# An output projection over 448 rows instead of 512, with half-row passes of paired token tiles, and the transfers that go with it

## The chip, the cores and the metric

The kernel runs on one NeuronCore of one Trainium2 chip. TensorE (PE) multiplies matrices and writes its results to PSUM, in banks of 128 partitions by 512 floats. ScalarE (ACT), VectorE (DVE) and GpSimd (POOL) do elementwise work, and SyncE (SP) issues almost all DMA transfers. Each engine carries out its own instructions in order, and the engines meet at semaphores. The metric is device time in microseconds (us); lower is better.

## The reference

Two kinds of layers alternate, each applied twice with the same weights, on 2048 tokens of 448 features:

```python
B, S, D, H = 1, 2048, 448, 16          # Dh = D // H = 28
def _A_ref(x, wq, wk, wv, wo):
    q = (x @ wq).reshape(B, S, H, Dh).transpose(0, 2, 1, 3)
    k = x @ wk                          # one key and one value head for all 16
    v = x @ wv
    p = softmax(einsum("bhqd,bkd->bhqk", q, k) * Dh ** -0.5)
    o = einsum("bhqk,bkd->bhqd", p, v)
    return o.transpose(0, 2, 1, 3).reshape(B, S, H * Dh) @ wo
def _B_ref(x, w_gate, w_up, w_down):    # w_gate, w_up: 448 x 1792
    return (silu(x @ w_gate) * (x @ w_up)) @ w_down
x = x + _A_ref(layernorm(x), wq, wk, wv, wo)
x = x + _B_ref(layernorm(x), w_gate, w_up, w_down)
x = x + _A_ref(layernorm(x), wq, wk, wv, wo)
x = x + _B_ref(layernorm(x), w_gate, w_up, w_down)
```

The change concerns the last line of `_A_ref`, the product with `wo`, whose contraction runs over 16 heads of 28 rows, 448 in all.

## The kernel before

**Tiling.** The 2048 tokens are 16 tiles of 128, four of which make a chunk `c` of 512. The 16 heads are four groups `g` of four heads. `xres` holds the residual stream, one 448-wide row per token. Where an operand of a matmul needs float precision it is split into a high and a low half (`split`, L135 and L136: two GpSimd instructions), and a product takes three passes: high by high, high by low, low by high.

**Projection stage** (`Attention.project`, `q`). Per chunk, four products of 11 matmuls give queries, keys and values; 16 such products a layer, numbered by `self.seen` (0 to 15, called the first to the sixteenth below). ScalarE copies each result to a staging tile (L538, L539), SyncE stores it (`qd`, L540; `kt`, L543). `self.plan[n, 0]` and `self.plan[n, 1]` hold steps that are emitted before and after product n, and `self.when[n]` further steps behind it: the loads of keys (`key_load`), the stacking of queries (`stack`, L421) and their halving (`parts`). Before each chunk's first products its normalized input is turned by TensorE (`flip`, L248) and halved. `norm_steps` gives the steps of a normalization: four statistics on VectorE (L217, L218), the reciprocal root on GpSimd (`scale`, L222 and L223), four applications on VectorE (L230). In layer 0 the statistics of chunks 2 and 3 are taken together behind the fifth product (`chunks=2`).

**Attention stage** (`scores`). For each of 16 pairs (chunk, head group), called `i`, there are eight cycles `u`, each of two key tiles. In a cycle TensorE computes the scores of both tiles with four heads side by side in 32-row strips (`tile_scores`, L605): three heads go into a triple of PSUM banks (`threes[0]` for the first tile, `threes[1]` for the second), the fourth into a single bank. ScalarE takes the exponentials out of the triples (L627), VectorE copies the single banks (L626), ScalarE takes the exponentials of these (L628). Then TensorE multiplies the previous cycle's exponentials by the values, four heads in 32-column strips (`pv`, L660), and VectorE adds the result to `accs[i]` (L667 at u = 0, L669 after). A column of ones among the values leaves the softmax sum in row 28 of each head's 32 rows.

**After a group** (`post`). SyncE collects the sums (`rs`, L683). Four cycles later, at u = 3 of the next pair, `rest` takes reciprocals (L691), sends them through DRAM and back to all rows (L693, L694), multiplies on GpSimd (L701), and halves the result into `onh` and `onl`. Here each group has 128 rows, of which 4 x 28 count: the projection contracts 4 x 128 = 512 rows, and `load_wo` places wo in the same layout over zeros.

**Output projection** (`outproj`). For a token tile of 128 there are 4 groups by 3 passes, 12 matmuls of 128 rows by 448 columns (L590). For chunks 0, 1 and 2 this is done between two cycles (`between_cycles`, at u = 6, as soon as the chunk's last group is halved): token tiles 1, 2 and 3 into `threes[0]`, then three additions to `xres` (L594), then tile 0 into a single bank and its addition. For chunk 3 it follows the attention stage, between the first units of the feed-forward: `rest` is called behind `unit(0, 0, 0)`, three groups are projected ahead of the remaining step of the down product, the last group after it.

**Feed-forward** (`FeedForward.unit`). Per chunk and 128 hidden features: two products into two of the banks 0 to 3 (`LOW`), silu on ScalarE (L953), a product on VectorE (L954), halving (L955, L958), and the down product (`down`) in 64-row halves side by side (`side_by_side`, L332).

**Between the layers** (`hand_over`). In the last group of units each chunk is normalized for layer 1, turned on VectorE (L268), sent to DRAM (L274), loaded in the other layout (L882 to L885) into two of the three query stacks `qts`, free at that time, and halved. For chunk 2 the halving stands in `plan[6, 0]` of layer 1.

A variant of `forward` for large scores (`full`) is compiled too and runs only if a check of the sums fails.

Of the kernel before, what the change touches and what calls it, by code (L numbers as in the profile page):

```python
# [55 lines left out]
def forward(  # L56
# [84 lines left out]
    halfn = pers.tile([P, 8], F32, name="halfn")  # L141
# [69 lines left out]
    def norm_steps(c, pool=pers, twice=True, chunks=1):  # L211

        got = {}
        cs = slice(4 * c, 4 * c + 4 * chunks)
# [5 lines left out]
        def scale():  # L220
            rstd = pers.tile([P, 4 * chunks], F32, name=f"rstd{chunks}", bufs=2)
            nc.gpsimd.tensor_scalar(rstd, mv[:, cs, 1], 1.0, EPS, ALU.mult, ALU.add)  # L222
            nc.gpsimd.tensor_tensor(rstd, rstd, halfn[:, 0 : 4 * chunks], ALU.pow)  # L223
            got["r"] = rstd
# [9 lines left out]
        fs = [lambda t=t: stat(t) for t in range(4 * chunks)] + [scale]  # L234
# [108 lines left out]
    class Attention:  # L343
# [222 lines left out]
        def scores(self, ff, xb):  # L566
            next(switch)
            inner = ExitStack()
            with tc.tile_pool(name=f"ow{self.layer}", bufs=1, side="right", reuse_waits="tile") as ow:
# [4 lines left out]
                on, accs, pts = {}, {}, {}  # L574
                todo, due, late = [], {}, []

                def load_wo(z):
                    r = wpool.tile([P, 4, 2, P], F32, name="wr").rearrange("p (z k) b n -> p z (k b n)", z=2)
                    nc.gpsimd.memset(r, 0.0)
                    for j in range(4):  # L580
                        nc.sync.dma_start(r[32 * j : 32 * j + DH, :, 0:D], wos[j][:, 2 * z : 2 * z + 2, :])
                    zs = slice(2 * z, 2 * z + 2)
                    split(woh[:, zs, :], wol[:, zs, :], r[:, :, 0:D])

                def outproj(c, t, po, gs=range(NG)):
                    oh, ol = on[c]
                    ts_ = slice(P * t, P * t + P)
                    for g in gs:
                        for z, (a, b) in enumerate(((oh, woh), (oh, wol), (ol, woh))):
                            nc.tensor.matmul(  # L590
                                po[:, 0:D], a[:, g, ts_], b[:, g, :], start=(g + z == 0), stop=(g == NG - 1 and z == 2)
                            )
                    if gs[-1] == NG - 1:
                        return lambda: nc.vector.tensor_tensor(  # L594
                            xres[:, 4 * c + t, :], po[:, 0:D], xres[:, 4 * c + t, :], ALU.add
                        )
# [38 lines left out]
                def between_cycles(m):  # L635
# [7 lines left out]
                    if not todo or u != 6:  # L643
                        return
                    c = todo.pop()
                    one = singles(m)[1]
                    adds = []
                    for t in (1, 2, 3):
                        adds.append(outproj(c, t, threes[0][:, t - 1, :]))
                    for f in adds:  # L650
                        f()
                    outproj(c, 0, one)()

                def pv(m, to):
# [18 lines left out]
                    if u == NT // 2 - 1:  # L673
                        due[m + 4] = post(i)

                def post(i):
# [5 lines left out]
                    for j in range(4):  # L682
                        nc.sync.dma_start(rs[32 * j : 32 * j + 32, :], oraw[32 * j + DH : 32 * j + DH + 1, :])  # L683

                    def rest():
# [9 lines left out]
                        if g == 0:  # L695
# [3 lines left out]
                            )  # L699
                        oh, ol = on[c]  # L700
                        nc.gpsimd.tensor_tensor(rb, oraw, rb, ALU.mult)  # L701
# [4 lines left out]
                    return rest  # L706
# [72 lines left out]
                for gs in (range(NG - 1), range(NG - 1, NG)):  # L779
                    for t in range(4):  # L780
                        add = outproj(NC - 1, t, pos[t], gs)
                        if add:
                            add()
                    while ff.left:
# [324 lines left out]
```

## Time and profile before

| what | value |
|---|---|
| median of 3 runs | 1973.64 us (1972.16 to 1973.9) |
| the profiled execution | 1973.03 us, of which the span from first to last instruction is 1971.3 us |
| granted TensorE clock, mean | 0.996 of full speed |
| TensorE busy | 1943.9 us (99%) |
| ScalarE busy | 1260.6 us (64%) |
| VectorE busy | 967.6 us (49%) |
| GpSimd busy | 554.1 us (28%) |
| DMA | 80.50 MB in 99875 packets |
| projection matmuls (L590) | 216 into triples, 168 into single banks |

A timeline row has the start in us from the span's start, the duration in us, the engine, the line of the kernel, the operation, the tile written and the tiles read, and the count; in brackets the engine's idle time before it and what ended that idle time. SPq rows are transfers as SyncE issues them. Rows of the chain of waits have start, duration, and engine or transfer. A row of windows has the stretch, its length, each engine's busy time and count (PE, PEld, DVE, ACT, POOL), the granted clock, the DMA share and GB/s. A matmul's duration is its passage through a pipeline; the distance between the starts of two matmuls is what one costs.

### The profile page before, as it was taken

The numbers are of one execution on the slowest core, as the hardware profiler recorded it, in microseconds if no ns is written. First come the engines' busy times: TensorE is split into PE (matmuls) and PEld (weight loads), VectorE is DVE, ScalarE is ACT, GpSimd is POOL, SyncE is SP. The second block draws the span as 40 slices with busy tenths as digits, with TensorE's granted clock in tenths as the row PEclk, the third lists the DMA queues.
The fourth block names the chain that finished last, engine by engine and source line by source line (L and its number), as shares of the span: only waits on it lengthen the run. The fifth ranks groups of instructions, "written<-read, shape, count | busy, mean of one in ns | idle before, by whom it ended". The sixth has DMA issues, their size and how long they took to land.

```text
span 1971.3 us, 43781 instructions
## 1 busy us (share of the span) xinstructions
PE 1943.9 (99%) x18469; PEld 1340.4 (68%) x18469; DVE 967.6 (49%) x1638; ACT 1260.6 (64%) x1888; POOL 554.1 (28%) x595
## 2 busy tenths in 40 slices
PE   8999999999999999999989999999999999999998
PEld 6644545445458999999965445454454689988886
DVE  6565575665744232322655565656657432222223
ACT  3799798997963333333348997979979433333332
POOL 4313123122214233333332221122221243233320
PEclk9999999999999999999999999999999999999999
DMA  4201002021130111100251010200211300011102
GB/s 152 68 23 33 18 23 52 17 52 32 28 74 22 32 32 32 32 21 23 70 149 40 26 31 12 61 14 23 51 49 26 75 17 27 21 32 32 32 1 77
DMA packets 99875, 80.50 MB, mean 41 GB/s; under 512 B 25848, under 2 KB 82296, under 8 KB 99672
## 3 DMA queue, kind: packets, MB, share of 16 engines
q1 hardware_dynamic: 98120, 76.44, 14.2%
q8 instruction: 146, 2.39, 0.5%
q10 hardware_dynamic: 1552, 1.20, 0.2%
q14 instruction: 57, 0.47, 0.1%
HBM read 56.24 MB, written 20.58 MB: 39 GB/s over the span
## 4 chain that ended last, share of the span: by engine, by line
PE 95%; DVE 1%; DMA 1%; POOL 1%; ACT 1%; issue 1%; SPq 0%; ACTq 0%; POOLq 0%; DVEq 0%
PE bank L332 40%; PE bank L660 24%; PE bank L605 17%; PE three L605 5%; PE bank L312 3%; PE three L590 2%; PE bank L590 2%; PE bank L248 1%; DMA kt<-stage 0%; PE bank L438 0%; DVE stats L217 0%; DMA xd<-xh 0%; POOL vsb L549 0%; DMA xres<-in_A_x_dram 0%; DVE pair L626 0%
## 5 line engine op out<-in xcount | busy, mean ns | idle before, releaser
L627 ACT ACTIVATE pt<-three 128x1536 f32<-128x1536 f32 x512 | 727.2, 1500 | 63.5 <-PE three L605 42.3
L660 PE MATMUL bank<-pt,vsb 128*32 128x512 f32 x3072 | 490.8, 598 | 0.4
L660 PE MATMUL bank<-pair,vsb 128*32 128x512 f32 x1024 | 487.4, 598 | 0.6 <-ACT pair L628 0.6
L605 PE MATMUL bank<-qstack,keys 32*128 32x512 f32 x1536 | 473.1, 424 | 4.3 <-DVE xres L594 4.3
L605 PE MATMUL three<-qstack,keys 32*128 32x512 f32 x4608 | 428.3, 408 | 0.5 <-ACT stage L539 0.3
L605 PEld LDWEIGHTS bank<-qstack,keys 32*128 32x128 f32 x1536 | 243.8, 183 | 255.9 <-issue 123.9
L332 PE MATMUL bank<-xh,wgh 64*128 64x512 f32 x1728 | 405.5, 387 | 0.0
L626 DVE COPY pair<-bank 128x512 f32<-128x512 f32 x512 | 354.3, 692 | 99.3 <-PE bank L605 62.4
L332 PE MATMUL bank<-xh,wgl 64*128 64x512 f32 x1404 | 340.8, 386 | 0.0
L332 PE MATMUL bank<-wdh,h 64*128 64x448 f32 x1792 | 322.4, 362 | 1.4 <-ACT h L955 0.8
L954 DVE TENSOR_TENSOR sg<-bank,sg 128x512 f32<-128x512 f32 x112 | 77.5, 692 | 493.6 <-ACT sg L953 489.4
L332 PE MATMUL bank<-xl,wgh 64*128 64x512 f32 x1296 | 303.3, 386 | 0.0
L628 ACT ACTIVATE pair<-pair 128x1024 f32<-128x1024 f32 x256 | 285.5, 1115 | 0.0
L605 PEld LDWEIGHTS three<-qstack,keys 32*128 32x128 f32 x4608 | 261.2, 183 | 12.7 <-ACT stage L539 0.7
L660 PEld LDWEIGHTS bank<-pt,vsb 128*32 128x32 f32 x3072 | 101.7, 109 | 246.7 <-issue 153.2
L837 POOL TENSOR_TENSOR xres<-stage,xres 128x448 f32<-128x448 f32 x108 | 126.1, 1186 | 495.9 <-ACT stage L836 495.7
L669 DVE TENSOR_TENSOR o<-bank,o 128x512 f32<-128x512 f32 x224 | 155.0, 692 | 204.2 <-PE bank L660 204.2
L339 ACT COPY seen<-bank 128x1 f32<-128x1 f32 x664 | 78.7, 164 | 251.8 <-PE bank L332 250.4
L332 PEld LDWEIGHTS bank<-xh,wgh 64*128 64x128 f32 x1728 | 225.7, 184 | 13.7 <-issue 1.3
L332 PEld LDWEIGHTS bank<-wdh,h 64*128 64x128 f32 x1792 | 217.7, 183 | 13.0 <-issue 2.0
L953 ACT ACTIVATE sg<-bank 128x512 f32<-128x512 f32 x112 | 67.1, 599 | 213.2 <-PE bank L332 210.5
L332 PE MATMUL bank<-wdl,h 64*128 64x448 f32 x896 | 199.1, 364 | 0.0
(134 smaller groups left out, 2193.7 us busy)
## 6 DMA issues: line engine op xcount, KB each, us to landing
o<-rd SPq DMA_DIRECT2D x32, 256.0 KB
qraw<-qd SPq DMA_DIRECT2D x128, 56.0 KB
qd<-stage SPq DMA_DIRECT2D x28, 224.0 KB
wdr<-in_B_w_down_dram SPq DMA_DIRECT2D x28, 224.0 KB
xt<-tb SPq DMA_DIRECT2D x24, 224.0 KB
wr<-in_B_w_gate_dram SPq DMA_DIRECT2D x28, 192.0 KB
wr<-in_B_w_up_dram SPq DMA_DIRECT2D x28, 192.0 KB
xn<-xt SPq DMA_DIRECT2D x6, 768.0 KB
```

The source lines that it names most:

```text
L332: nc.tensor.matmul(po, a, b, start=start, stop=stop, skip_group_check=True)
L339: nc.scalar.copy(seen[:, i : i + 1], po[:, 0:1])
L590: nc.tensor.matmul(po[:, 0:D], a[:, g, ts_], b[:, g, :], start=(g + z == 0), stop=(g == NG - 1 and z == 2))
L605: nc.tensor.matmul(three[:, j, :] if j < 3 else one, k[js, kp, ks], q[js, part, :], start=(z == 0), stop=(z == 2), tile_position=(32 * j, 0),)
L626: copies.append(nc.vector.tensor_copy(pt1, one))
L627: es.append(nc.scalar.activation(pt, threes[y], AF.Exp, scale=SCALE))
L628: es.append(nc.scalar.activation(pair, pair, AF.Exp, scale=SCALE))
L660: nc.tensor.matmul(to[32 * j : 32 * j + 32, :], vsb[:, n % NT, :], pts[n][j], start=(y == 0), stop=(y == 1), skip_group_check=True,)
L669: f = nc.vector.tensor_tensor(accs[i][:, 0, :], to, accs[i][:, 0, :], ALU.add)
L837: nc.gpsimd.tensor_tensor(r, s, r, ALU.add)
L953: nc.scalar.activation(in_order(sg, sq), natural(pg[0], sq), AF.Silu)
L954: nc.vector.tensor_tensor(in_order(sg, sq), natural(pg[1], sq), in_order(sg, sq), ALU.mult)
```

## The change

- **Layout.** Group 0 keeps 64 rows: two of its heads with eight rows in their gaps. The other 56 - 8 = 48 rows of its other two heads go into the gaps (4 of every 32 rows) of groups 1, 2 and 3, which are then full. A copy of group 0's 64 rows stands in partitions 64 to 127. `load_wo` places wo accordingly, row by row range, with 8 transfers per group and without the zero fill.
- **Passes.** `half_rows` takes group 0 for two token tiles at once, one on partitions 0 to 63 and one on 64 to 127, into two banks; `full_rows` takes groups 1 to 3 for one token tile. In `between_cycles` (now at u = 7) the four tiles stand in both triples, two each; the halves of all four come first, then the full rows in an order that alternates between the triples, each tile's addition behind its last matmul.
- **Spreading.** `post` returns three steps instead of one: `rest` (u = 3) up to the multiplication, `spread` (u = 4), which moves the rows by transfers (for group 0 to a DRAM tile `moved` and from there into its own gaps, then the copy of the 64 rows; for the other groups four transfers out of `moved`), and `parts` (u = 6), which halves. At the end of attention `rest` comes ahead of `unit(0, 0, 0)`, `spread` and `parts` behind it. The sums are collected by one transfer instead of four.
- **Layer 0's normalization** is per chunk throughout; chunk 3's statistics come behind product 8.
- **Layer 1's projection.** The turned chunks are loaded into `qts[1]` and `qts[2]` instead of `qts[0]` and `qts[1]`; chunk 2's load moves behind product 4 and its halving from ahead of product 6 to ahead of product 7.

```diff
...
-    def norm_steps(c, pool=pers, twice=True, chunks=1):
+    def norm_steps(c, pool=pers, twice=True):
...
                 def load_wo(z):
-                    r = wpool.tile([P, 4, 2, P], F32, name="wr").rearrange("p (z k) b n -> p z (k b n)", z=2)
-                    nc.gpsimd.memset(r, 0.0)
-                    for j in range(4):
-                        nc.sync.dma_start(r[32 * j : 32 * j + DH, :, 0:D], wos[j][:, 2 * z : 2 * z + 2, :])
+                    r = wpool.tile([P, 4, 2, P], F32, name="wr").rearrange("p (z k) b n -> p z (k b n)", z=2)[:, :, 0:D]
+                    for g in (2 * z, 2 * z + 1):
+                        s_ = r[:, g % 2, :]
...
+                        own = wo[4 * DH * g : 4 * DH * g + 4 * DH, :]
+                        n0 = 2 * DH + 16 * g - 16
+                        for q in range(4):
+                            nc.sync.dma_start(s_[32 * q : 32 * q + DH, :], own[DH * q : DH * q + DH, :])
+                            nc.sync.dma_start(s_[DH + q :: 32, :], wo[n0 + 4 * q : n0 + 4 * q + 4, :])
...
+                def full_rows(c, t, po, gs):
+
                     for g in gs:
-                        for z, (a, b) in enumerate(((oh, woh), (oh, wol), (ol, woh))):
+                        for z, (a, b) in enumerate(passes(c)):
                             nc.tensor.matmul(
-                                po[:, 0:D], a[:, g, ts_], b[:, g, :], start=(g + z == 0), stop=(g == NG - 1 and z == 2)
+                                po[:, 0:D], a[:, g, P * t : P * t + P], b[:, g, :],
+                                start=False, stop=(g == NG - 1 and z == 2), skip_group_check=True,
                             )
...
+                def half_rows(c, ts, pos):
+
+                    for z, (a, b) in enumerate(passes(c)):
+                        for t, po, rs in zip(ts, pos, (slice(0, 64), slice(64, 128))):
+                            nc.tensor.matmul(
+                                po[:, 0:D], a[rs, 0, P * t : P * t + P], b[rs, 0, :],
+                                start=(z == 0), stop=False, skip_group_check=True,
+                            )
...
-                    if not todo or u != 6:
+                    if not todo or u != 7:
                         return
                     c = todo.pop()
-                    one = singles(m)[1]
-                    adds = []
-                    for t in (1, 2, 3):
-                        adds.append(outproj(c, t, threes[0][:, t - 1, :]))
-                    for f in adds:
-                        f()
-                    outproj(c, 0, one)()
+                    order = (1, 2, 3, 0)
+                    pos = [threes[n // 2][:, n % 2, :] for n in range(4)]
+                    for n in (0, 2):
+                        half_rows(c, order[n : n + 2], pos[n : n + 2])
+                    for n in (0, 2, 1, 3):
+                        full_rows(c, order[n], pos[n], range(1, NG))
+                        add_to(c, order[n], pos[n])()
...
-                        due[m + 4] = post(i)
+                        rest, spread, parts = post(i)
+                        due[m + 4], due[m + 5], due[m + 7] = rest, spread, parts
...
-                    for j in range(4):
-                        nc.sync.dma_start(rs[32 * j : 32 * j + 32, :], oraw[32 * j + DH : 32 * j + DH + 1, :])
+                    nc.sync.dma_start(rs, oraw[DH::32, :].rearrange("j (p n) -> j p n", n=16))
...
+                    def spread():
+                        if g == 0:
+                            moved[c] = dram.tile([2 * DH, 512], F32, name=f"moved{self.layer}_{c}")
+                            for q in (0, 1):
+                                nc.sync.dma_start(moved[c][DH * q : DH * q + DH, :], rb[64 + 32 * q : 64 + 32 * q + DH, :])
+                            for q in (0, 1):
+                                n0 = 2 * DH - 8 + 4 * q
+                                nc.sync.dma_start(rb[32 * q + DH : 32 * q + 32, :], moved[c][n0 : n0 + 4, :])
+                            nc.sync.dma_start(rb[64:128, :], rb[0:64, :])
+                            return
+                        n0 = 16 * g - 16
+                        for q in range(4):
+                            nc.sync.dma_start(rb[DH + q :: 32, :], moved[c][n0 + 4 * q : n0 + 4 * q + 4, :])
...
                 ff.begin(xb)
+                due.pop(min(due))()
                 ff.unit(0, 0, 0)
-                due.popitem()[1]()
+                due.pop(min(due))()
                 ff.fetch(2)
+                due.pop(min(due))()
                 ff.unit(0, 0, 1)
-                pos = [bank(LOW)[1] for _ in range(4)]
...
+                c, pos = NC - 1, [bank(LOW)[1] for _ in range(4)]
+                for two in (slice(0, 2), slice(2, 4)):
+                    half_rows(c, range(4)[two], pos[two])
+                for t in range(4):
+                    full_rows(c, t, pos[t], range(1, NG - 1))
+                while ff.left:
+                    ff.left.pop(0)()
+                for t in range(4):
+                    full_rows(c, t, pos[t], range(NG - 1, NG))
+                    add_to(c, t, pos[t])()
...
             if c == 2:
-                a.plan[6, 0] = [parts]
+                a.plan[4, 1] = [load]
+                a.plan[7, 0] = [parts]
                 return
...
-        if c == 2:
-            two = got
-            at.plan[n, 1] = fs[:9]
-        elif c == 1:
-            at.plan[n, 1] = fs[:5]
-        else:
-            at.plan[n, 1] = [lambda got=got: got.__setitem__("r", two["r"][:, 4:8])]
-        at.plan[n + 1, 1] = fs[-4:] + [lambda c=c, got=got: at.norms.__setitem__(c, got)]
+        at.plan[n, 1] = fs[:5]
+        at.plan[n + 1, 1] = fs[5:] + [lambda c=c, got=got: at.norms.__setitem__(c, got)]
```

More of the change, by code (lines that the diff above doesn't have):

```diff
@@ L220, in scale @@
         def scale():
-            rstd = pers.tile([P, 4 * chunks], F32, name=f"rstd{chunks}", bufs=2)
+            rstd = pers.tile([P, 4], F32, name="rstd", bufs=2)
             nc.gpsimd.tensor_scalar(rstd, mv[:, cs, 1], 1.0, EPS, ALU.mult, ALU.add)
-            nc.gpsimd.tensor_tensor(rstd, rstd, halfn[:, 0 : 4 * chunks], ALU.pow)
+            nc.gpsimd.tensor_tensor(rstd, rstd, halfn, ALU.pow)
             got["r"] = rstd
@@ L232, in apply @@
                 nc.gpsimd.tensor_copy(got["x"][:, t, D:512], o[:, 384:D])
-        fs = [lambda t=t: stat(t) for t in range(4 * chunks)] + [scale]
+        fs = [lambda t=t: stat(t) for t in range(4)] + [scale]
         return fs + [lambda t=t: apply(t) for t in range(4)], got
```

50 lines of the change are left out of this document (27 added, 23 removed).

## The prediction

> **What bounds the kernel now.** I read the list of engines first, then the chain that ended last.
>
> ```profile
> PE 1943.9 (99%) x18469; PEld 1340.4 (68%) x18469; DVE 967.6 (49%) x1638; ACT 1260.6 (64%) x1888; POOL 554.1 (28%) x595
> PE 95%; DVE 1%; DMA 1%; POOL 1%; ACT 1%; issue 1%; SPq 0%; ACTq 0%; POOLq 0%; DVEq 0%
> ```
>
> TensorE is the path: 95% of the chain. A change gains by taking slots from TensorE or by closing one of its few holes. So I looked up every place that the diff touches in the timeline and read it there. All durations are from the profiled execution, which took 1973.03 us, 0.6 below the median of 1973.64.
>
> **Part 1: the six projections inside attention.** This is TensorE at the second of them, from its first matmul to the scores behind it.
>
> ```profile
> 337.57 0.47 PE L590 MATMUL three<-woh,onh 128*128 128x448 f32 x1
> 337.88 0.36 PE L590 MATMUL three<-wol,onh 128*128 128x448 f32 x1
> ...
> 347.19 0.37 PE L590 MATMUL bank<-woh,onl 128*128 128x448 f32 x1
> 347.60 0.62 DVE L594 TENSOR_TENSOR xres<-bank,xres 128x448 f32<-128x448 f32 x1 [0.67 <-PE bank L590]
> 348.28 0.49 PE L605 MATMUL bank<-qstack,keys 32*128 32x512 f32 x1 [0.72 <-DVE xres L594]
> ...
> 349.33 2.79 ACT L627 ACTIVATE pt<-three 128x1536 f32<-128x1536 f32 x2 [10.61 <-PE bank L605]
> ```
>
> Starts count here, not durations, because matmuls overlap. 48 matmuls: 0.31 to the second start, 46 steps of (347.19 - 337.88) / 46 = 0.2024, and 1.09 to the scores, 0.72 of it a wait for the last addition. Together 10.71 us. ScalarE stands idle for 10.61 of them, so a shorter projection is a shorter span: ScalarE gives nothing back.
>
> The change runs 64 rows instead of 128 for a quarter of the contraction, two token tiles side by side: 48 slots become 36 full and 6 paired. No row shows a paired slot in this place; the feed-forward's down product has the same shape, and behind it stands a switch from 64 to 128 rows.
>
> ```profile
> 978.08 0.41 PE L332 MATMUL bank<-wdl,h 64*128 64x448 f32 x2
> 978.28 0.41 PE L332 MATMUL bank<-wdh,h 64*128 64x448 f32 x2
> 978.62 0.50 PE L312 MATMUL bank<-xh,wh 128*128 128x512 f32 x1
> 978.96 0.40 PE L312 MATMUL bank<-xl,wh 128*128 128x512 f32 x1
> ```
>
> A pair takes 0.20. The switch takes 0.34 for 0.20, and then 0.34 for the 0.23 of a matmul of 512 columns (10.02 us for 44, quoted in part 4): 0.25 extra, once per projection. The wait of 0.72 goes: the next scores write a triple whose last addition began nine full slots earlier, and a bank that the projection no longer uses. Late next is the other triple: its last addition ends 0.41 + 0.62 = 1.03 after the last matmul's start, and the second tile's scores come about 0.37 + 0.8 = 1.17 after it. That hides it by 0.14; uncovered it costs a few tenths. New length: 0.31 + 40 x 0.2024 + 0.37 + 0.25 = 9.03. Gain 1.68, times six: **10.1 us**. Bounds: 2.8 if pairs take two slots each (6 x 6 x 0.20 back), 11.6 if the switch is free.
>
> **Part 2: the transfers in front of it.** Rows of a group are now spread by SyncE between the product with the reciprocals and the halving, and the projection comes one cycle later.
>
> ```profile
> 199.60 0.49 PE L605 MATMUL bank<-qstack,keys 32*128 32x512 f32 x1
> 205.98 1.28 POOL L701 TENSOR_TENSOR o<-o 128x512 f32<-128x512 f32 x1 [7.83 <-DMA o<-rd]
> 206.87 0.49 PE L605 MATMUL bank<-qstack,keys 32*128 32x512 f32 x1
> 207.35 0.62 POOL L135 TENSOR_SCALAR onh<-o 128x512 fp32r<-128x512 f32 x1
> 208.06 1.29 POOL L136 TENSOR_TENSOR onl<-o,onh 128x512 fp32r<-128x512 f32 x1
> 989.09 2.99 DMA kt<-stage
> 1026.84 5.43 DMA kt<-stage
> 593.02 2.31 DMA xd<-xh
> ```
>
> 199.60 is the start of cycle u = 4 and 206.87 that of u = 6, so a cycle is 3.63. The product ends at 207.3. Four small transfers, 0.5 each to issue and 2.3 to land (the nearest row, xd), end at 211.6; the halving, 1.9, at 213.5. The projection now starts at 214.1, needing the last group 2.7 later. Hidden, with 3 to spare. Behind the waiting SyncE stand the next group's transfers and, in two groups, a load of the normalized input; behind the waiting GpSimd, the next query halves, five cycles away. In the first group of a chunk three transfers follow each other: 207.3 + 5 x 0.5 + 3 x 2.3 + 1.9 = 218.6. Its buffer is needed again at about 221.5, when VectorE copies the next but one group's first sum. Hidden, with 2.9 to spare. Loading wo takes 64 transfers instead of 16 and no memset; nothing waits. This part: **0**.
>
> The Trainium skill, "DMA: Bandwidth & Descriptors", section "Anatomy of one DMA", puts about 2.0 us of fixed cost on each transfer, whatever its size (measured there on the software path). It speaks against splitting as the change does; by it the three take 6 us, still hidden, while the rows above go from 2.3 to 5.4.
>
> **Part 3: the projection of the last chunk, once per layer.** Six slots less are 1.21. But the first halves come at once.
>
> ```profile
> 580.84 0.47 PE L590 MATMUL bank<-woh,onh 128*128 128x448 f32 x1
> 581.76 0.69 DVE L954 TENSOR_TENSOR sg<-bank,sg 128x512 f32<-128x512 f32 x1 [4.15 <-ACT sg L953]
> 589.74 0.47 PE L590 MATMUL bank<-woh,onh 128*128 128x448 f32 x1
> ```
>
> The second pair of tiles writes the banks of the unit just computed, which VectorE frees at 582.45; the pair is due at about 581.4. So 1.1 of 1.21 is a new wait. The reciprocals are now issued ahead of the first unit, which pays for the spread: product at about 582, last group ready at about 589, needed at about 589.6 (589.74, less 1.21, plus 1.1). I take **0.2 us** for both layers; bounds -3 (the chain 1.5 late each time) and 2.4.
>
> **Part 4: the first projection stage.** Normalization of chunks 2 and 3 is no longer joined. That looks like tidying; the trace says otherwise.
>
> ```profile
> 29.01 0.62 DVE L217 BATCH_NORM_STATS2 stats<-xres 128x6 f32<-128x448 f32 x1
> 34.77 0.18 DVE L218 BATCH_NORM_AGGREGATE mv<-stats 128x2 f32<-128x6 f32 x1
> 35.40 1.64 POOL L223 TENSOR_TENSOR rstd<-rstd,halfn 128x8 f32<-128x8 f32 x1
> 37.08 1.78 DVE L230 TENSOR_SCALAR xn<-xres,mv,rstd 128x448 f32<-128x448 f32 x4 [2.13 <-POOL rstd L223]
> 37.65 4.30 PE L248 MATMUL bank<-ident,xn 128*128 128x128 f32 x16 [2.52 <-DVE xn L230]
> 37.60:42.00 4.40, 4.36 (x17) 3.63 (x18) 4.18 (x9) 1.78 (x4) 1.43 (x4) 0.50 0.01 2
> 41.95 10.96 PE bank L312 x44
> 52.91 0.94 PE bank L438 x4
> 53.84 1.75 PE bank L248 x16
> 55.59 10.02 PE bank L312 x44
> ```
>
> Eight tiles of statistics run from 29.01 to 34.95, GpSimd's power follows, and the flips of chunk 2 wait 2.52 for the input that VectorE then normalizes. Meanwhile the granted clock falls to 0.50 (third figure from the end of the window's row): the flips take 4.30 where the next chunk's take 1.75, and 44 matmuls 10.96 instead of 10.02. With four tiles the input is normalized from 37.08 - 2.97 - 0.62 (a smaller power) = 33.5 on, done by 35.3. The wait goes but for 0.3, and with it the slow clock, 2.55 in the flips and 0.94 behind them. What is late next is chunk 3: its four statistics, 3.0, now come after the ninth product. The flips of chunk 3 would be due at about 35.1 + 1.75 + 10.0 + 0.9 = 47.8. On VectorE the statistics stand behind chunk 2's splits and a transpose and end at about 44.7; GpSimd has a key halving ahead of the power, which ends at about 46.6; four normalizations end at 48.4. About 0.4 is lost. Gain 2.2 + 2.55 + 0.94 - 0.4 = **5.3 us**; bounds 2 (the wait less the loss) and 6.
>
> **Part 5: the second projection stage.** The largest hole that I found:
>
> ```profile
> 997.13 0.59 ACT L539 COPY stage<-bank 128x512 f32<-128x512 f32 x1
> 1006.19 0.38 SPq L882 DMA_DIRECT2D qstack<-xt  x1
> 1008.29 1.05 SPq L540 DMA_DIRECT2D qd<-stage  x2
> 1012.38 0.59 ACT L539 COPY stage<-bank 128x512 f32<-128x512 f32 x1 [5.07 <-DMA qd<-stage]
> 1015.45 0.69 DVE L302 TENSOR_TENSOR xh<-qstack,xh 64x512 fp32r<-64x512 f32 x1
> 1017.03 0.76 PE L312 MATMUL bank<-xh,wh 128*128 128x512 f32 x1 [5.75 <-DVE sg L440]
> 1021.03 0.39 PE L312 MATMUL bank<-xh,wh 128*128 128x512 f32 x1
> ```
>
> SyncE waits at chunk 2's load (L882) until the sent chunk has landed, with the fourth product's store, ready at 997.7, behind it until 1008.29. ScalarE therefore gets its staging buffer only at 1012.38, chunk 2's halves are done at 1016.1, and the ninth product, 11 matmuls, runs from 1017.03 to 1021.03, 4.0 instead of 11 x 0.228 = 2.5, since the clock had dropped again. Moved behind the fifth product, the load lets that store out at about 1003 but itself goes out at about 1007.8 instead of 1006.2. It lands near 1012 (2.3 behind the last issue at 1009.8); ScalarE's sixth and seventh copies no longer wait for the late store; VectorE has by then done the maxima that now stand ahead of the halves, and ends at about 1015.5. The products can start on the first rows from 1012.5, so the ninth ends at 1016.1 at full clock, about 1017 if it drops again. I take 1017: **4.0 us**. Bounds: 0 (the later load eats it) and 6.
>
> The Trainium skill, "TensorE: Matmul & The Clock Gate", Part 1, halves the clock only after an idle window of about 3.4 us. By it this shorter hole would not slow the clock and 0.9 more is gained; but the waits of part 4, 2.52 us, were enough for 0.50.
>
> **Sum.** 10.1 + 0 + 0.2 + 5.3 + 4.0 = 19.6, and 1973.03 - 19.6 = 1953.4 in a profiled execution; the median stood 0.6 above that of before, and I give **1953.5**.
>
> **Rivals.**
> - *The spread is late (slower).* One place: the first group of a chunk, eight times. Three transfers in a row have 221.5 - 207.3 - 2.5 - 1.9 = 9.8 us, 3.3 each. Below that nothing; at the 5.43 of the slow store quoted, 6.5 late, with VectorE held in its copy and TensorE's next product behind it: 8 x 6.5 - 20 = 32 slower, 2005. For it: the store at 2.99 is near the limit. Against: loads and copies in this trace land at 2.3 to 2.7. 8%.
> - *The halves do not run side by side:* 8 x 6 x 0.20 = 9.7 back, 1963. Against: the pairs at 978.08. 6%.
> - *The second stage gains nothing:* the load is the late one, 1957.5. 13%.
> - *The chain of part 3 is late:* 3 us, 1956.5. 7%.
> - *More is gained,* clock up throughout and free switches: 1948.5 to 1950. 6%.
>
> **How the numbers follow.** The forecast, with 1950 to 1956 as its own range, has 60%. All rivals but the first end faster: 0.90, since 0.02 goes to a spread so little late that the gain is just eaten, within 0.2% (about what a measurement of this kernel can tell from no change); 0.08 slower. The range reaches to the serial halves above, 1964, and below to all upper bounds at once, 1973 - (11.6 + 2.4 + 6 + 6) = 1947.
>
> **What would show it.** Right: 42 steps of 0.20 and no wait for an addition at the scores; flips of chunk 2 near 35 at clock 1.00; the ninth product of layer 1 ending four earlier relative to its stage. Wrong: VectorE's first copy of a sum waiting for GpSimd; TensorE waiting in the projection for GpSimd's halves; SyncE's late stores now elsewhere in the second stage, with a new hole at a later product.

## The result, and the profile after

The change took the kernel from 1973.64 us to 1962.54 us (medians of six runs each, 1972.08 to 1974.0 and 1961.99 to 1963.64). The ratio is 0.9945, with a 95% interval of 0.9934 to 0.9955. The gain is 11.1 us, where 20.1 had been forecast. The profiled execution after took 1962.25 us with a span of 1960.4. This is its list of engines, and the first line of the chain that ended last:

```profile
PE 1943.3 (99%) x18469; PEld 1325.5 (68%) x18469; DVE 968.3 (49%) x1638; ACT 1264.1 (64%) x1888; POOL 553.6 (28%) x593
PE 87%; ACT 9%; DMA 1%; DVE 1%; issue 1%; POOL 0%; SPq 0%; ACTq 0%; POOLq 0%; DVEq 0%
```

TensorE is still the path. But its busy time has hardly fallen (1943.9 to 1943.3), although each layer's projections have lost slots. Something else on TensorE got longer. A table of leads shows where: for one place in the program after the other, its time from the start of the span in both traces, and how far the changed kernel is ahead.

| place | before | after | lead |
|---|---|---|---|
| first scores, layer 0 | 69.00 | 63.71 | 5.3 |
| first silu of the feed-forward, layer 0 | 572.06 | 561.13 | 10.9 |
| its third silu (last chunk's projection done) | 599.43 | 588.62 | 10.8 |
| its last silu but one | 977.50 | 970.78 | **6.7** |
| first scores, layer 1 | 1042.73 | 1032.85 | 9.9 |
| first silu of the feed-forward, layer 1 | 1545.80 | 1530.39 | 15.4 |
| its third silu | 1573.15 | 1557.89 | 15.3 |
| its last silu | 1958.89 | 1947.76 | **11.1** |
| end of the span | 1971.31 | 1960.42 | 10.9 |

Every stage that the diff touches gains about what was forecast. Both feed-forwards, in which the diff has not changed a line, lose 4.1 us each. The loss is spread evenly. Here are two silus of the feed-forward's units, 29 units apart, in the timeline of ScalarE; first the kernel before:

```profile
761.10 0.60 ACT L953 ACTIVATE sg<-bank 128x512 f32<-128x512 f32 x1 [1.93 <-PE bank L332]
...
970.28 0.60 ACT L953 ACTIVATE sg<-bank 128x512 f32<-128x512 f32 x1 [1.98 <-PE bank L332]
```

and after:

```profile
759.27 0.60 ACT L1006 ACTIVATE sg<-bank 128x512 f32<-128x512 f32 x1 [2.15 <-PE bank L332]
...
970.78 0.60 ACT L1006 ACTIVATE sg<-bank 128x512 f32<-128x512 f32 x1 [1.96 <-PE bank L332]
```

(970.28 - 761.10) / 29 = 7.213 us a unit before, (970.78 - 759.27) / 29 = 7.293 after. Layer 1 has the same two lengths. Some 105 units at 0.08 us are 8.4 us, nearly all of the 9.0 us by which the gain fell short.

Next, the rows of after that answer those shown of before. The second projection inside attention:

```profile
333.97 0.47 PE L621 MATMUL three<-woh,onh 64*128 64x448 f32 x2
334.28 0.36 PE L621 MATMUL three<-wol,onh 64*128 64x448 f32 x2
...
342.60 0.37 PE L612 MATMUL three<-woh,onl 128*128 128x448 f32 x1
342.89 0.50 PE L633 MATMUL bank<-qstack,keys 32*128 32x512 f32 x1
...
343.00 0.62 DVE L604 TENSOR_TENSOR xres<-three,xres 128x448 f32<-128x448 f32 x1 [1.20 <-PE three L612]
343.95 2.79 ACT L655 ACTIVATE pt<-three 128x1536 f32<-128x1536 f32 x2 [8.82 <-PE three L633]
```

From the first pair (x2: both halves in one row) to the scores it is 342.89 - 333.97 = 8.92 instead of 10.71. The scores wait for nothing: the last addition (343.00) runs beside them. ScalarE is idle for 8.82 instead of 10.61.

The first projection stage: VectorE's normalization of chunk 3 and TensorE's flips of chunks 2 and 3, then the granted clock under the flips of chunk 2 (1.00, third figure from the end):

```profile
34.83 2.08 PE L248 MATMUL bank<-ident,xn 128*128 128x128 f32 x16
...
46.37 1.78 DVE L230 TENSOR_SCALAR xn<-xres,mv,rstd 128x448 f32<-128x448 f32 x4 [1.57 <-POOL rstd L223]
47.70 2.15 PE L248 MATMUL bank<-ident,xn 128*128 128x128 f32 x16
```

```profile
34.80:37.00 2.20, 2.20 (x19) 1.94 (x18) 2.06 (x5) 2.20 (x5) 0.71 (x3) 1.00 0.50 158
```

The flips of chunk 2 start 2.8 us earlier, at full clock, and take 2.08 instead of 4.30. Those of chunk 3 take 2.15 instead of 1.75, because the four normalizations end only at 46.37 + 1.78 = 48.15.

The second projection stage, around its ninth product:

```profile
1001.10 0.39 SPq L934 DMA_DIRECT2D qstack<-xt  x1
...
1005.43 1.88 ACT L292 CAST xh<-qstack 128x512 fp32r<-128x512 f32 x3 [2.27 <-DMA qstack<-xt]
1006.10 0.50 PE L312 MATMUL bank<-xh,wh 128*128 128x512 f32 x1 [1.72 <-ACT xh L292]
...
1010.59 0.61 PE L312 MATMUL bank<-xh,wh 128*128 128x512 f32 x1
1011.02 0.42 PE L312 MATMUL bank<-xl,wh 128*128 128x512 f32 x1
...
1024.18 0.50 PE L312 MATMUL bank<-xh,wh 128*128 128x512 f32 x1 [0.47 <-DVE vt L546]
```

TensorE's wait is 1.72 us (5.75 before). The load is now what it waits for. Behind this short wait the matmuls still go at a distance of 0.43 instead of 0.23 until 1011.02 in this execution. The last row is a wait that the kernel before did not have: at the fourteenth product TensorE waits 0.47 us for VectorE's copy of the values (`vt`).

### The profile page after: what moved, and what is told of

Same layout as the page of the kernel before. It is cut to its first block, busy times and chain, and to the rows that moved or that the text cites. A ratio compares the mean times of both kernels' runs of the same rounds, so it can differ in the third digit from the quotient of the medians.

```text
span 1960.4 us, 44004 instructions
## 1 busy us (share of the span) xinstructions
PE 1943.3 (99%) x18469; PEld 1325.5 (68%) x18469; DVE 968.3 (49%) x1638; ACT 1264.1 (64%) x1888; POOL 553.6 (28%) x593
## 4 chain that ended last, share of the span: by engine, by line
PE 87%; ACT 9%; DMA 1%; DVE 1%; issue 1%; POOL 0%; SPq 0%; ACTq 0%; POOLq 0%; DVEq 0%
PE bank L332 40%; PE bank L688 20%; PE bank L633 14%; ACT pt L655 6%; PE three L633 5%; PE bank L312 4%; ACT pair L656 2%; PE three L612 2%; PE bank L612 1%; PE three L621 0%; PE bank L438 0%; DMA kt<-stage 0%; DMA xd<-xh 0%; DMA wr<-in_A_wq_dram 0%; DVE vt L546 0%
## 5 line engine op out<-in xcount | busy, mean ns | idle before, releaser
L332 PE MATMUL bank<-xh,wgh 64*128 64x512 f32 x1728 | 450.7, 389 | 0.0
L332 PE MATMUL bank<-xh,wgl 64*128 64x512 f32 x1404 | 371.7, 391 | 0.0
L332 PE MATMUL bank<-xl,wgh 64*128 64x512 f32 x1296 | 338.1, 390 | 0.0
L332 PE MATMUL bank<-wdh,h 64*128 64x448 f32 x1792 | 334.3, 364 | 1.1 <-ACT h L1008 0.8
L656 ACT ACTIVATE pair<-pair 128x1024 f32<-128x1024 f32 x256 | 281.5, 1100 | 0.0
L332 PEld LDWEIGHTS bank<-xh,wgh 64*128 64x128 f32 x1728 | 266.3, 185 | 16.7 <-issue 1.3
L332 PEld LDWEIGHTS bank<-wdh,h 64*128 64x128 f32 x1792 | 247.5, 184 | 14.8 <-issue 2.0
L332 PEld LDWEIGHTS bank<-xh,wgl 64*128 64x128 f32 x1404 | 219.2, 184 | 13.8
L332 PE MATMUL bank<-wdl,h 64*128 64x448 f32 x896 | 222.2, 367 | 0.0
```

What stands on the lines that cost most here:

```text
L332: nc.tensor.matmul(po, a, b, start=start, stop=stop, skip_group_check=True)
L656: es.append(nc.scalar.activation(pair, pair, AF.Exp, scale=SCALE))
```

## The experiments

**First theory, and its fall.** In the middle of the feed-forward the upper 64 rows run 0.12 us behind the lower ones before the change (starts at 728.21 and 728.33) and 0.20 after (718.65 and 718.85; both streams go through `side_by_side`). I supposed at first that the streams now enter the feed-forward out of step and that this costs 0.08 us a unit. The traces contradict it without a run. In layer 1 the streams fall into step; here is the last pair of a unit before the change and one after it, lower half (xh) and upper half (xd):

```profile
1832.34 0.39 PE L332 MATMUL bank<-xh,wgl 64*128 64x512 f32 x1
1832.34 0.39 PE L332 MATMUL bank<-xd,wgl 64*128 64x512 f32 x1
```

```profile
1863.56 0.39 PE L332 MATMUL bank<-xh,wgl 64*128 64x512 f32 x1
1863.56 0.39 PE L332 MATMUL bank<-xd,wgl 64*128 64x512 f32 x1
```

Both halves start together in both kernels, and the unit there is still 7.21 before (silus at 1829.05 and 1836.26) and 7.29 after (1860.24 and 1867.53). So the distance of the streams doesn't set the length.

**Second theory: placement.** In the feed-forward the instructions, their order and their PSUM banks are the same in both programs. What differs is where the operands lie in SBUF. The joint normalization had a wide tile, `rstd2` (two buffers of 32 bytes a partition); with it gone, everything allocated behind it (silu buffer, feed-forward weights, inputs) lies 64 bytes lower, while the split silu products `h2`, allocated ahead of it, stay. (No trace shows addresses. The 64 bytes follow from the order and the sizes of the allocations; for the second run below they hold only if every tile takes a multiple of 32 bytes.) The theory: this shift makes the unit longer. The rival: something in the way the feed-forward is entered, or the added transfers.

*Putting 64 bytes back, in the changed kernel:*

```diff
             rstd = pers.tile([P, 4], F32, name="rstd", bufs=2)
+            if c == 2:
+                pers.tile([P, 16], F32, name="room")
```

> The changed kernel with 64 bytes a partition of unused SBUF put back where the removed wide normalization tile lay, so that weights, inputs and silu products of the feed-forward lie at the addresses that they had before the change; its instructions stay those of the changed kernel. Placement theory: the feed-forward's unit of work goes back from 7.293 us (changed kernel) to 7.213 us (before) in both layers, and with some 107 units at 0.08 us the time falls by 8.5 us to about 1954. Rival (the unit is longer because of how the two row halves of TensorE enter the feed-forward, or because of the additional transfers, or by where the instructions lie): the unit stays at 7.293 us and the time at 1962.5 within 1 us.

Measured: 1953.85 us (ratio to the kernel before 0.9901, interval 0.9885 to 0.9918).

```profile
757.97 0.60 ACT L1008 ACTIVATE sg<-bank 128x512 f32<-128x512 f32 x1 [2.06 <-PE bank L334]
...
967.16 0.60 ACT L1008 ACTIVATE sg<-bank 128x512 f32<-128x512 f32 x1 [1.93 <-PE bank L334]
```

209.19 / 29 = 7.213. An unused tile, to which no instruction refers, gives 8.7 us.

*Taking 64 bytes away, in the kernel before:*

```diff
-            rstd = pers.tile([P, 4 * chunks], F32, name=f"rstd{chunks}", bufs=2)
+            rstd = pers.tile([P, 8], F32, name="rstd", bufs=2)[:, 0 : 4 * chunks]
```

> The kernel before the change, whose two normalization tiles take one name and together 64 bytes a partition less, so that the feed-forward's tiles lie where the changed kernel has them; nothing else differs. Placement theory: the unit of the feed-forward becomes 7.293 us and the time rises by 8.5 us to about 1982. Rival (entry of the row halves, transfers, instructions): unit 7.213 us, time 1973.6 within 1 us.

Measured: 1981.77 us (1.0044, interval 1.0027 to 1.0061).

```profile
761.65 0.60 ACT L953 ACTIVATE sg<-bank 128x512 f32<-128x512 f32 x1 [1.96 <-PE bank L332]
...
973.15 0.60 ACT L953 ACTIVATE sg<-bank 128x512 f32<-128x512 f32 x1 [2.14 <-PE bank L332]
```

211.50 / 29 = 7.293. The two runs together show the cause: the shift, put back in the one kernel and made in the other, moves the unit between the two lengths, and the times follow. The traces agree slot by slot too: averaged over 19 units, the 33 distances between pairs are the same within 0.001 us in the kernel before and in the changed one with 64 bytes, and again in the changed one and in the kernel before with 64 bytes less; between these two groups some differ by 0.009.

*Other amounts of room* (`[P, 8]` and `[P, 32]` in the first diff):

> The changed kernel with 32 bytes of unused SBUF at that place. Placement theory: another unit length may come out here, since every operand changes its place modulo 64 bytes; if the length follows the place modulo 64 alone, this differs from both lengths seen, and room for 64 bytes would equal none. Rival (not placement): 7.293 us and 1962.5.

> The changed kernel with 128 bytes of unused SBUF at that place. Placement theory with a period of 128 bytes: unit 7.293 us, as without room. Placement theory with a longer period or with the distance to the tiles that do not move (the split silu products): 7.213 us or a third length. Rival (not placement): 7.293 us and 1962.5, told from the first by the run with 64 bytes.

Measured once each: 1964.95 us with 32 bytes, 1952.91 with 128. First 32 bytes, then 128 (the rows are of the later run with the same kernel, 28 units apart):

```profile
760.13 0.60 ACT L1008 ACTIVATE sg<-bank 128x512 f32<-128x512 f32 x1 [2.15 <-PE bank L334]
...
972.41 0.60 ACT L1008 ACTIVATE sg<-bank 128x512 f32<-128x512 f32 x1 [1.97 <-PE bank L334]
```

```profile
757.77 0.60 ACT L1008 ACTIVATE sg<-bank 128x512 f32<-128x512 f32 x1 [2.00 <-PE bank L334]
...
959.37 0.60 ACT L1008 ACTIVATE sg<-bank 128x512 f32<-128x512 f32 x1 [2.00 <-PE bank L334]
```

212.28 / 29 = 7.320 and 201.60 / 28 = 7.200. No period of 64 or 128 bytes: 0 and 128 give different lengths.

*Which distances count.* 64 bytes between the weights and the inputs, and 64 bytes ahead of `h2`, so that everything moves together:

```diff
     xpool = ctx.enter_context(tc.tile_pool(name="xpool", bufs=1))
+    xpool.tile([P, 16], F32, name="room")
```

> The changed kernel with the 64 bytes of unused SBUF put behind the feed-forward's weights and ahead of its inputs: inputs (xh, xl, xd) lie as before the change, weights and silu products as in the changed kernel. If the place of the inputs alone sets the slots, the unit is 7.213 us and the time 1953.9; if the place of the weights alone, 7.293 us and 1962.5; if what counts is the place of one against the other, a third length, such as the 7.32 or 7.20 us that 32 and 128 bytes gave.

```diff
     seen = pers.tile([P, 4], F32, name="seen")
+    pers.tile([P, 16], F32, name="room")
```

> The changed kernel with the 64 bytes put ahead of the split silu products (h2) too, so that everything the feed-forward's multiplications read moves together. If the place in the partition itself counts, it comes out as with room behind h2: 7.213 us and 1953.9. If the distance from the silu products to weights and inputs counts, nothing has changed: 7.293 us and 1962.5.

Measured once each: 1964.18 and 1961.52 us.

```profile
762.65 0.60 ACT L1007 ACTIVATE sg<-bank 128x512 f32<-128x512 f32 x1 [2.13 <-PE bank L333]
...
973.96 0.60 ACT L1007 ACTIVATE sg<-bank 128x512 f32<-128x512 f32 x1 [1.97 <-PE bank L333]
```

```profile
759.15 0.60 ACT L1007 ACTIVATE sg<-bank 128x512 f32<-128x512 f32 x1 [2.14 <-PE bank L332]
...
970.65 0.60 ACT L1007 ACTIVATE sg<-bank 128x512 f32<-128x512 f32 x1 [1.96 <-PE bank L332]
```

Inputs alone: 211.31 / 29 = 7.287, a length of its own (its time is also longer because in that execution TensorE waited 2.92 us at its first product, and the first scores came at 67.29). All together: 211.50 / 29 = 7.293, as without room. So the place itself doesn't count, at least not for 64 bytes: what counts is how far apart the operands lie. Moving the inputs alone gave neither of the two lengths, so more than one distance counts; which ones these runs don't separate.

Where inside a unit is it? TensorE's pairs of one half unit, changed kernel first, then with 64 bytes:

```profile
694.48 0.58 PE L332 MATMUL bank<-xh,wgh 64*128 64x512 f32 x2
...
695.87 0.57 PE L332 MATMUL bank<-xh,wgh 64*128 64x512 f32 x2
...
696.77 0.40 PE L332 MATMUL bank<-xh,wgl 64*128 64x512 f32 x1
```

```profile
693.95 0.52 PE L334 MATMUL bank<-xh,wgh 64*128 64x512 f32 x2
...
695.31 0.52 PE L334 MATMUL bank<-xh,wgh 64*128 64x512 f32 x2
...
696.22 0.39 PE L334 MATMUL bank<-xh,wgl 64*128 64x512 f32 x1
```

The first six slots take 1.39 us against 1.36, the next four 0.90 against 0.91. So most of the excess sits behind the switch from the down product (which reads `h2`) to gate and up, and dies out: two such places make 0.06 of the unit's 0.08 (0.028 each in the average over 19 units), and nearly all of the rest is the slot ahead of each down product (0.237 against 0.228). By what rule a distance lengthens a slot remains open; moving the weights alone wasn't tried.

**The terms of the prediction, one at a time.** All but one of these stand on the changed kernel with 64 bytes of room (1953.85), so that the feed-forward doesn't mix in.

*Halves not side by side:*

```diff
-                        for t, po, rs in zip(ts, pos, (slice(0, 64), slice(64, 128))):
+                        for t, po, rs in zip(ts, pos, (slice(0, 64), slice(0, 64))):
```

> The changed kernel with 64 bytes of room, and both halves of a pair multiplied in the lower 64 rows (the same data lies in both), so that they follow each other instead of lying side by side. By the prediction's reason (42 slots of 0.20 us instead of 48, because six pairs lie side by side) each of the eight output projections gets six slots longer: 8 x 6 x 0.20 = 9.6 us, about 1963.5. Rival (halves were never side by side, the gain came from the alternation of the banks alone): no change, 1953.9.

Measured: 1962.05 us, 8.2 more.

```profile
209.31 0.56 PE L623 MATMUL three<-wol,onh 64*128 64x448 f32 x2
209.72 0.56 PE L623 MATMUL three<-woh,onl 64*128 64x448 f32 x2
```

A pair now takes 0.41 (209.72 - 209.31), and 0.20 side by side (334.28 against 334.48 in the changed kernel). Each attention stage is 3.8 us longer, 1.28 a projection, and each last chunk's projection only 0.4: TensorE waits there for a bank anyway (0.27 and 0.26 with the halves side by side, 0.18 without). The rival falls.

*Full rows triple by triple:*

```diff
-                    for n in (0, 2, 1, 3):
+                    for n in (0, 1, 2, 3):
```

> The changed kernel with 64 bytes of room, and the full rows of the four token tiles taken triple by triple (first both of the one, then both of the other) instead of alternately. If multiplications into one bank of a triple wait until VectorE has added the other bank of it, each of the six projections in attention waits twice for an addition of 0.62 us and its release: 6 x 2 x 0.7 = 8.4 us, about 1962. If waits are kept bank by bank, the additions lie beside the multiplications either way: 1953.9.

Measured: 1966.24 us, 12.4 more, all of it in attention (6.2 and 6.5 us). The longest line in TensorE's list of waits (us in total, times, longest), and one of the waits:

```profile
PE three L614 <- DVE xres L606: 9.4, 12, 0.8
```

```profile
340.04 0.62 DVE L606 TENSOR_TENSOR xres<-three,xres 128x448 f32<-128x448 f32 x1 [2.79 <-PE three L614]
340.72 0.47 PE L614 MATMUL three<-woh,onh 128*128 128x448 f32 x1 [0.79 <-DVE xres L606]
```

A matmul into one bank of a triple does wait for the addition that reads the other. Twelve waits of 0.79 are 9.4; the remaining 3 us are the restarts, 0.25 each. The alternation is worth more than the halves: without it the attention stages would be 0.6 and 0.9 us longer than before the change.

*The joint normalization put back* (the only one without room: the wide tile comes back with it):

```diff
+            rstd = pers.tile([P, 4 * chunks], F32, name=f"rstd{chunks}", bufs=2)
...
+        fs, got = norm_steps(c, chunks=2 if c == 2 else 1)
```

> The changed kernel with the joint normalization of the chunks 2 and 3 put back, and with it the wide tile of 64 bytes (no other room). By the prediction's terms alone the first projection stage loses 5.3 us and nothing else moves: 1967.8. With the placement theory the tile gives the feed-forward its old place back, 8.5 us, so that undoing this part makes the kernel faster: 1962.5 + 5.3 - 8.5 = about 1959.3, unit 7.213 us.

Measured: 1957.63 us, 4.9 *less* than the changed kernel, and a unit of 7.213. Undoing a part that gains makes the kernel faster, because its tile was worth more than its time. Against the changed kernel with room it costs 3.8, not 5.3. The flips and the wait ahead of them are those of before the change (4.29 after 2.52). But the 44 matmuls behind them take less, 9.99 instead of 10.96, by the chain of waits:

```profile
41.83 9.99 PE bank L312 x44
```

The windows from 35 to 45 us say why, by the granted clock; before the change first, then this kernel:

```profile
35.00:45.00 10.00, 7.48 (x27) 5.96 (x27) 7.29 (x14) 3.11 (x6) 5.87 (x12) 0.66 0.20 64
```

```profile
35.00:45.00 10.00, 7.29 (x32) 6.09 (x32) 7.28 (x14) 3.63 (x8) 5.98 (x12) 0.83 0.22 72
```

At half clock for a time t, the mean over 10 us is 1 - 0.5 t / 10: t is 6.8 us before and 3.4 here. The same wait drew two slow stretches in the one execution and one in the other.

*The second projection's transfers as before:*

```diff
-            raw = [q.bitcast(F32)[:, z, :] for q in qts[1:] for z in range(2)]
+            raw = [q.bitcast(F32)[:, z, :] for q in qts[:2] for z in range(2)]
...
-                if c < 2:
-                    load()
...
-                a.plan[4, 1] = [load]
-                a.plan[7, 0] = [parts]
+                a.plan[6, 0] = [parts]
```

> The changed kernel with 64 bytes of room and the second projection's transfers as they were before the change (chunk 2's load issued in its turn, into the first stack, its split one place earlier). By the prediction's term for that stage: 4.0 us slower than with room alone, about 1957.9; by what the two traces showed (52.51 us before, 49.4 after), 3.1 us: 1957.0. The stall ahead of the ninth product is back at 5.7 us. Rival (the stage gained nothing by its transfers, only by other parts): 1953.9.

Measured: 1957.26 us, 3.4 more. The old hole is back:

```profile
1006.13 0.76 PE L314 MATMUL bank<-xh,wh 128*128 128x512 f32 x1 [5.77 <-DVE sg L442]
```

*The spread one step later:*

```diff
-                        due[m + 4], due[m + 5], due[m + 7] = rest, spread, parts
+                        due[m + 4], due[m + 6], due[m + 7] = rest, spread, parts
```

> The changed kernel with 64 bytes of room, and the transfers that spread each group's four surplus heads issued one step of the cycle (3.63 us) later. The prediction put their margin at 2.9 to 3.0 us: 0.6 to 0.7 us a group would then be late at VectorE's next copy into the buffer, up to 32 x 0.7 = 22 us in both layers if nothing else takes it up, 0 if VectorE's copies may be late. Rival of the prediction (transfers already late in the changed kernel): all of the 3.6 us shows, 32 x 3.6 = 115 us. Transfers with more margin than I read: 1953.9.

Measured: 1953.59 us, no change, but the run doesn't answer the question. SyncE issues the transfers at the same time as without the edit; the first row is without it, the second with it:

```profile
202.50 2.12 SPq L744 DMA_DIRECT2D o<-moved  x4
```

```profile
202.55 2.12 SPq L744 DMA_DIRECT2D o<-moved  x4
```

In both, SyncE stands there waiting for GpSimd's product (it ends at 202.47 and 202.52), and nothing of SyncE's own lies between the two places. The edit moved the instruction in the text and not in time, so the margin of 3 us stays untested from this side.

*The best version, timed:*

> The changed kernel with 128 bytes of room once more, timed against the kernel before in rounds: the single run gave 1952.91, the unit 7.200 us against 7.213 with 64 bytes. 107 units at 0.0133 us make 1.4 us: about 1952.4 if 64 bytes give 1953.85. If the single run was chance: the same as with 64 bytes.

Measured: 1953.09 us, ratio to the kernel before 0.9898 (0.9882 to 0.9915). It and the version with 64 bytes (1953.85) beat both kernels by 8.7 us or more; between the two of them lie 0.8 us.

## Why the prediction was right, and where it was wrong

The direction held. The time lies inside the outer range of 1947 to 1964, but that is luck: the upper end was set by halves one after the other, which did not come true. The narrower range of 1950 to 1956 was missed, and the time is 9.0 us above 1953.5. **The step that failed is the sum**: "10.1 + 0 + 0.2 + 5.3 + 4.0 = 19.6" has no term for the feed-forward. It took 770 us of the span as untouched because no instruction there is touched. The runs show in its place a loss of 8.2 us between the two traces, 8.7 by the run with 64 bytes, from a tile of 64 bytes that disappears in the very part 4 that I priced by its time alone. With the old distances the changed kernel takes 1953.85, and 1953.5 had been forecast. That these two agree so closely is luck in part: in the trace with 64 bytes the attention stages gain 1.1 more than forecast, and the two projection stages 0.5 and 0.9 less, the last chunks' projections 0.3 less. That the measured 1962.54 lies near the rival of halves one after the other (1963) is chance: that rival's own experiment excludes it.

Point by point, each against its own stage:

- **Part 1, 10.1 us.** Right in mechanism, a little low. A projection is 8.92 long, 9.03 forecast; six times 1.79 are 10.7, and the two attention stages gained 11.2 in all (5.65 and 5.53); where the other 0.5 comes from I have not traced. Pairs cost 0.20, and the last addition lies beside the scores, as said. What the working took for granted, that the additions are hidden, hangs on the order of the triples: 12.4 us.
- **Part 2, nothing.** Right: no row has TensorE waiting in a projection for the halves. In the first groups of a chunk, for which a margin of 2.9 had been forecast, the halves end 4.0 to 5.6 ahead of VectorE's next copy into that buffer. The smallest margins, 2.7 to 3.0, are in third groups, of which the prediction had no term: one has its halves done at 184.21, behind the split of wo, and the copy starts at 187.17. How much lateness they bear wasn't shown.
- **Part 3, 0.2 us gained.** About 0.3 lost (from the first to the third silu 27.37 and 27.35 before, 27.49 and 27.50 after); with 64 bytes of room it comes to 0.06 lost. The new wait at the banks is there:

```profile
570.23 0.37 PE L621 MATMUL bank<-woh,onl 64*128 64x448 f32 x2
570.87 0.47 PE L621 MATMUL bank<-woh,onh 64*128 64x448 f32 x1 [0.27 <-ACT sg L1006]
571.60 0.47 PE L621 MATMUL bank<-woh,onh 64*128 64x448 f32 x1 [0.25 <-DVE sg L1007]
```

  The second pair's upper half comes 1.37 after the pair ahead instead of 0.20: 1.2, forecast 1.1.
- **Part 4, 5.3 us.** Right between the two traces (69.00 to 63.71), down to the 0.4 lost at chunk 3 (2.15 instead of 1.75). But undoing the part costs 3.8. Of the difference, 1.1 lies between two executions of the old steps, which wait the same 2.52: the profiled one of before had one slow stretch more (first scores at 69.00) than the experiment (67.88). The rest is scatter of this stage (63.71 in the one execution of the changed code, 64.23 in the other). The term took for fixed what one execution had drawn.
- **Part 5, 4.0 us.** 3.2 between the traces, 3.4 by undoing it. The load goes out 29.2 us after the stage's first matmul (971.90) and the ninth product ends 38.7 after it, forecast 38.4. So the product itself ends 3.7 earlier, and 0.5 is given back behind it: 0.2 by the next product's first matmul, which is still slow (1010.59 to 1011.02), the rest by the new wait of 0.47 at the fourteenth product. I had let the slow clock end with the ninth product. But the clock matters less than I thought: in the execution with 64 bytes TensorE waits 1.54 and 0.40 here, the clock stays at 1.00 and the tenth product starts 37.4 after the first matmul instead of 38.7; the scores come no earlier (61.03 after it, against 60.95), because the wait for `vt` is then 1.35.
- **The signs** of being right came as named: steps of 0.20, no addition waited for, flips of chunk 2 at 34.83 at full clock, the ninth product 3.7 earlier relative to its stage (42.4 before). One sign of being wrong came too, in part: the new wait at the fourteenth product, ahead of which ScalarE's copy to the staging tile (at 1022.73) waits 0.88 for a store of keys.

## What to carry to other kernels

A diff that adds, removes or resizes a tile also moves every tile behind it; compare the repeated unit of the stages that it doesn't touch, to a hundredth of a microsecond, before crediting or blaming the code. When touched stages gain as forecast and the total doesn't, put back the old addresses with an unused tile: it costs one run and parts code from placement. And before shortening a chain of matmuls, see whether the banks they write are tracked one by one or as one tile, since here the order over the two triples was worth more than the slots saved.

## What the runs showed of the hardware

- Matmuls on two 64-row halves take longer or shorter with the distance of their operands in SBUF: 7.200, 7.213, 7.287, 7.293 and 7.320 us for the same unit of 66 matmuls, with tiles moved by 32 to 128 bytes. Over the kernel's 112 units the spread is 0.12 x 112 = 13 us, 0.7% of the time and more than the 11.1 us that the change gained as it stood. Moving all operands together by 64 bytes left the unit at 7.293.
- A wait of 1.72 us on TensorE, with one of 0.22 behind it, was followed by slow matmuls (0.43 apart instead of 0.23) from 1007.62 to 1011.02, 3.4 us. After one and the same wait of 2.52 us the clock was at half for 6.8 us in one execution and for 3.4 in another. Two executions of the same kernel, with 128 bytes of room, differ even more. The first waited 1.30 and 0.60 at the ninth product of layer 1 and its clock was at half for 3.4 us; the second waited 1.70 and 0.23 and kept the full clock:

  ```profile
  1001.00:1011.00 10.00, 9.06 (x32) 7.14 (x33) 4.05 (x6) 5.27 (x10) 6.76 (x12) 0.83 0.57 162
  ```

  ```profile
  1001.00:1011.00 10.00, 8.43 (x34) 6.11 (x34) 4.15 (x7) 5.43 (x10) 6.39 (x12) 1.00 0.55 160
  ```

  So a slow stretch came here in pieces of 3.4 us, and whether none, one or two follow a wait of 1.3 to 2.5 us was not a matter of the code alone. The Trainium skill, "TensorE: Matmul & The Clock Gate", Part 1 ("What's actually happening"), says that the gate watches a free-running window of about 3.4 us, and that the clock falls after an idle one. A free-running window agrees with the pieces seen here and with their changing number; that the whole window must be idle doesn't, since TensorE waited for 2.52 us or less.
